# Larger DMA packets for the FFN weights in a fused attention and FFN kernel, with a new order of TensorE's work

## The chip, the cores and the metric

The kernel runs on one core of one Trainium2 chip. A core has five engines that run side by side and wait for each other through semaphores: TensorE (PE in the profile; its weight loads are listed as PEld) multiplies matrices, VectorE (DVE) and ScalarE (ACT) work element by element, GpSimd (POOL) does the same more slowly and also issues DMAs, and SyncE (SP) here issues DMAs only. Sixteen DMA engines move data between the chip's main memory and the on-chip memories. The metric is the device time of one execution in microseconds (us).

## What is computed

The reference, cut to what matters. Batch is 8, with 12 heads, 448 rows and 64 columns a head; d_model is 768 and d_ff 2048. The inputs are float32, and the kernel multiplies in bf16.

```python
def _attn_ref(q, k, v, w_pre, w_post):
    scale = 1.0 / np.sqrt(q.shape[-1])
    scores = scale * np.matmul(q, k.transpose(0, 1, 3, 2))
    scores = np.einsum('bhij,hg->bgij', scores, w_pre)
    scores = scores - np.max(scores, axis=-1, keepdims=True)
    attn = np.exp(scores)
    attn = attn / (np.sum(attn, axis=-1, keepdims=True) + 1e-09)
    attn = np.einsum('bhij,hg->bgij', attn, w_post)
    return np.matmul(attn, v).astype(np.float32)

def _moe_ref(x, w_in, w_out):
    h = np.maximum(x @ w_in, 0.0)
    return (h * h @ w_out).astype(np.float32)
```

The attention's output, 3584 rows (8 x 448) of 768 columns, is the `x` of the FFN.

## The kernel before

**Stages.** For each batch b the kernel transposes q and k on TensorE (T), multiplies them to scores (QK), copies the scores to `stage` on ACT or DVE, and has SP move them by DMA into `dring` (L875, one DMA for a chunk of 10 rows), in which the heads of 10 rows lie on the partitions. A matmul with `wk1` then mixes the heads (pre, L898), ACT takes the exponentials and their row sums (L915), DVE the reciprocals (L929), GpSimd folds them into the second mixing matrix `wk2s` (L936), and a second matmul mixes the heads again (post, L968), evacuated into `a2t`. After that come the product with v (AV, L1027, evacuated into `xt`), the first FFN matmul with `w_in_sb` (F1, L1075), relu (L1103, L1104) and square (L1113), and the second FFN matmul with `w_out_sb` (F2, L1192, and L1141 for the last two tiles), evacuated into `osb` and written out from GpSimd's queue (L1224).

The first 22 chunks of batch 0 skip the move through `dring`: DVE writes q, scaled by the head-mixing weights (L758), into the memory of `w_out_sb` (chunks 0 to 15) and of `h2t` (the others), and "direct" matmuls (L780) give the mixed scores at once. So w_out can be loaded only when the direct matmuls of chunks 0 to 15 are done.

**Queues.** GpSimd issues all loads of q, k (L585), v (L597) and the two weights (L623), because they convert float32 to bf16 on the way, and the output. `emit_load_w` (L607 to L633) issues the weights: i = 0 is w_in, i = 1 is w_out, each in four quarters j, and each quarter has a semaphore `sem_w[i][j]`. A quarter of w_in is 512 of its 2048 columns, issued as two DMAs of 256 columns over all six blocks of 128 rows. A quarter of w_out is four of its 16 blocks of 128 rows, issued as three DMAs of 256 of its 768 columns. An issue covers 128 partitions, and each (partition, block) pair is one run of 256 elements: 512 bytes in bf16. The first quarter of w_in is issued ahead of the loads of v for batch 0 and of q and k for batch 1, the other three behind them, w_out later among the folds. The list `chain` fixes the order of q, k and the weights on the queue; w_out's issues also stand behind certain pre units in the planner's order (`pre_at`).

**The order.** A planner in the kernel (class `_Plan`) decides, when the program is built, which engine does a task and in which order. TensorE's work is cut into 948 units in ten streams: 0 is T, 1 QK, 2 pre, 3 post, 4 AV, 5 direct, 6 and 7 F1, 8 and 9 F2. The string `ORDER` (L27) names, digit by digit, the stream from which TensorE takes its next unit, and within a stream the order is fixed. A position in this text is an index into that string, from 0. Each engine works strictly in its own order: an instruction that waits holds up all behind it. Where the planner expects a gap for TensorE in the first 60 us it fills part of it with matmuls on constant data that nothing reads (L554, "warm-up"). The planner knows DMAs by a rough model: the tuple `dma=(kind, work, packet)` gives a DMA's length and the time of one packet, both in ns, from which it works out how loads and moves slow each other (`dma_next`). Costs of instructions on an engine are tuples such as `{POOL: (850.0, 0.0)}`. These numbers set no time on the chip; they decide the order on the engines other than TensorE, and which of ACT and DVE evacuates.

Of the kernel before, what the change touches and what calls it, by code (L numbers as in the profile page):

```python
# [13 lines left out]
POOL = "pool"  # L14
# [10 lines left out]
DMA_END = {"move": 2800.0, "load": 2300.0}  # L25
INF = float("inf")
ORDER = (  # L27
    "0001510011055555555555155555513151555535533555555555335553200535555531155112555300333223"
    "1001244311412167663762727233636223717211636733221117433244226362717137637166116712276267"
    "3227933390120913922008122833833423811004111412283382238321812363637117261617337222444263"  # L30
    "3627173611671270022811833382238633673127442163672616733422767160002071718131812281382239"
    "1191339222919133933392244224193161336237117002261633737226126710027362126733702208183118"
    "1318223913911391339222442283381318331822244442136116227117163336227337220062236373117633"
    "6202071722009131911391139222838331833182224442219133931913392224442238138313831181162226"
    "7020273736126736211673372200623633713722009119113911192228183138333822281813382244444422"
    "8363162200732731631617131736222676376373372020821381244128382200911911191339339223922291"
    "9338118111833382224444233622617117362261761173362273376211673372193392229983338322882224"
    "44383338222838633667366776444776787667676767676876776798989988999988"
)


# [275 lines left out]
def bass_talking_heads_attention__then__ffn_squared_relu_kernel(  # L317
# [11 lines left out]
    F, FF = moe_w_in.shape  # L329
# [4 lines left out]
    NCH = -(-S // CH)  # L334
# [14 lines left out]
    NFT = F // 128  # L349
# [11 lines left out]
    with ExitStack() as es:  # L361
        def sb(name, shape, dtype):
            return es.enter_context(nc.sbuf_tensor(name, list(shape), dtype))
# [9 lines left out]
        NWP = 4  # L373
# [4 lines left out]
        WC = 256  # L378
# [13 lines left out]
        w_in_sb = sb("w_in_sb", [128, NFT, FF], DT.bfloat16)  # L392
        w_out_sb = sb("w_out_sb", [128, NFFT, F], DT.bfloat16)
# [212 lines left out]

        def emit_load_w(i, deps, quarters=range(NWP)):  # L607
            for j in quarters:
                nx = 2 if i == 0 else 3
                ts = w_of[(i, j)] = []  # L610
                for x in range(nx):
                    def fn(eng, en, j=j, x=x):
                        if i == 0:
                            c0 = j * (FF // NWP) + x * WC
                            src = bass.AP(moe_w_in.tensor, c0,
                                          [[FF, 128], [128 * FF, NFT], [1, WC]])
                            dst = w_in_sb[:, :, c0:c0 + WC]
                        else:
                            nt = NFFT // NWP
                            src = bass.AP(moe_w_out.tensor, j * nt * 128 * F + x * WC,  # L620
                                          [[F, 128], [128 * F, nt], [1, WC]])
                            dst = w_out_sb[:, j * nt:(j + 1) * nt, x * WC:(x + 1) * WC]
                        eng.dma_start(dst, src).then_inc(sem_w[i][j].handle, 16)  # L623

                    t = plan.add(
                        "ldw%d_%d_%d" % (i, j, x), POOL, fn, deps,
                        {POOL: (850.0 if i == 0 else 800.0, 0.0)},
                        (-2e5 if i == 0 and j == 0 else WPRIO + i) + j * 0.1, sem_w[i][j], 16,
                        after=[chain["t"]] + ([] if i == 0 else [
                            pre_at(min(24 + 2 * (3 * j + x), NCH - 1))]),  # L630
                        dma=("load", 2600.0 - 800.0 * i, 60.0))
                    chain["t"] = t
                    ts.append(t)  # L633

# [25 lines left out]
        def pre_at(g):  # L660
            return pre_of[g - g % NCP + g % NCP // 2 * 2]
# [574 lines left out]
        for b in range(B):  # L1236
            if b != 1:
                emit_load_qk(b)
            if b == 0:
                emit_load_w(0, [], range(1))  # L1240
            emit_T(b)
            if b == 0:
                t_wsmall = plan.add("wsmall", SP, fn_wsmall, [t_init, T_of[(0, 0, 0)]], {SP: (2600.0, 9500.0)}, -1e6,
                                    sem_w0, 48)

                t_wk1 = add("wk1", DVE, fn_wk1, [t_wsmall, t_mask], {DVE: (300.0, 400.0)}, -450.0)

                t_wk2 = add("wk2", DVE, fn_wk2, [t_wsmall, t_mask2], {DVE: (300.0, 400.0)}, -450.0)
                emit_load_qk(1)
                emit_load_w(0, [], range(1, NWP))  # L1250
                for a in range(3):
                    for c in range(NE):
                        emit_direct(c, (a, 3 + a))
                for c in range(0, NE - 1, 2):
                    emit_post(c)
                for c in range(NE, ND):
                    for ps_ in ((0, 1, 2), (3, 4, 5)):
                        emit_direct(c, ps_)
                    if c % 2:
                        emit_post(c - 1)  # L1260
# [8 lines left out]
            if b == 0:  # L1269
                emit_load_w(1, [dir_done[c] for c in range(NDW)])  # L1270
                emit_load_v(b)
            else:
                emit_load_v(b)
# [110 lines left out]
```

## Time and profile before

| What | Value |
|---|---|
| Three runs, us | 532.49, 532.8, 534.94 |
| Median, us | 532.8 |
| The profiled execution, us | 533.16 |
| Its span, first to last instruction, us | 531.4 |
| Granted TensorE clock | 1.000 |
| Loads of w_in: issues, KB each, median us from issue to landing | 8, 384, 16.0 |
| Loads of w_out: issues, KB each, median us from issue to landing | 12, 256, 8.1 |
| First and last issue of w_in, us | 10.1, 27.2 |
| First and last issue of w_out, us | 40.8, 67.9 |
| First matmul that reads w_in, us | 56.6 |
| First F2 matmul that reads w_out, us | 96.7 |
| Software DMA queue (all that GpSimd issues): packets, MB | 42816, 33.04 |
| Hardware DMA queue (moves into dring, last outputs): packets, MB | 45000, 36.86 |

Times within an execution count from the start of its span. Sizes are of the data as it is written, so in bf16 for the loads. The share of the DMA engines can pass 1, as packets of two queues overlap on one engine. "Issue" as the cause of a wait means that the engine waited for nothing that the profile shows; for TensorE that is mostly its own instructions, which are fetched by DMA in blocks of 16 KB (81 packets of the instruction queue).

### The profile page before, as it was taken

To read this page: it belongs to the slowest core of one execution; us is meant where nothing else is said; L and a number is where in the kernel's file an instruction comes from. 1 tells how busy PE (TensorE), PEld (TensorE's weight loads), DVE (VectorE), ACT (ScalarE), POOL (GpSimd) and SP (SyncE) were. 2 spreads that over 40 slices of the span, in tenths; PEclk is the share of its full clock that TensorE was granted. 3 is DMA by queue.
4 is the path that set the end of the run, shared out by engine and by line. 5 is a ranking of instruction groups with operands and counts; after the bars stand their busy time and mean duration, and the time that the engine had idled before them with its cause. 6 is when DMAs were issued, how large, how long until landed. Compare 5 with 4: busy or idle time off the path is not lost.

```text
span 531.4 us, 24004 instructions
## 1 busy us (share of the span) xinstructions
PE 514.6 (97%) x10033; PEld 321.2 (60%) x10033; DVE 401.0 (75%) x986; ACT 425.4 (80%) x1216; POOL 208.9 (39%) x404
## 2 busy tenths in 40 slices
PE   8999997899999999999989999999999999999997
PEld 3454765566767565566545665557655565567964
DVE  7986887788878769986879778986688777946530
ACT  4779997889989888979989988987979888986311
POOL 9933455332741256323641456213721333132000
PEclk9999999999999999999999999999999999999999
DMA  8999999755995379846993579727982558441003
GB/s 117 179 223 163 190 189 191 152 110 124 169 188 110 87 163 171 158 91 145 163 190 80 139 145 177 170 48 154 178 153 68 144 145 140 106 98 49 3 18 103
DMA packets 88210, 71.63 MB, mean 135 GB/s; under 512 B 13368, under 2 KB 85608, under 8 KB 88104
## 3 DMA queue, kind: packets, MB, share of 16 engines
q0 software_dynamic: 42816, 33.04, 39.9%
q1 hardware_dynamic: 45000, 36.86, 29.0%
q8 instruction: 81, 1.33, 1.0%
q10 hardware_dynamic: 288, 0.20, 0.1%
q14 instruction: 25, 0.20, 0.1%
HBM read 45.70 MB, written 11.01 MB: 107 GB/s over the span
## 4 chain that ended last, share of the span: by engine, by line
PE 88%; ACT 6%; DVE 2%; issue 2%; POOL 1%; DMA 1%; POOLq 0%; ACTq 0%
PE ps L1192 26%; PE ps L1075 26%; PE ps L968 8%; PE ps L898 8%; PE ps L1027 7%; PE ps L829 6%; PE ps L780 4%; ACT pring L915 3%; PE ps L683 2%; PE ps L1141 2%; ACT stage L447 1%; DMA qraw<-in_q_dram 1%; ACT a2t L447 1%; POOL qraw L585 1%; DVE a2t L448 1%
## 5 line engine op out<-in xcount | busy, mean ns | idle before, releaser
L915 ACT ACTIVATE pring<-ps 128x448 bf16<-128x448 f32 x360 | 191.4, 556 | 15.1 <-PE ps L898 8.4
L1075 PE MATMUL ps<-xt,w_in_sb 64*128 64x448 bf16 (+2 forms) x2112 | 167.3, 299 | 3.0 <-issue 1.6
L936 POOL TENSOR_TENSOR wk2s<-wk2b,rinv 128x120 bf16<-128x120 bf16 (+1 forms) x179 | 71.6, 403 | 212.7 <-DVE rinv L929 212.1
L1192 PE MATMUL ps<-w_out_sb,h2t 64*128 64x384 bf16 x1664 | 151.3, 323 | 1.2 <-DVE h2t L1113 1.2
L448 DVE CAST a2t<-ps 128x480 bf16<-128x480 f32 (+1 forms) x197 | 120.5, 639 | 21.4 <-PE ps L968 20.6
L1075 PEld LDWEIGHTS ps<-xt,w_in_sb 64*128 64x128 bf16 x2112 | 94.8, 94 | 53.1 <-issue 5.7
L448 DVE CAST stage<-ps 128x448 bf16<-128x448 f32 (+1 forms) x177 | 106.6, 618 | 16.7 <-PE ps L829 14.7
L447 ACT ACTIVATE stage<-ps 128x448 bf16<-128x448 f32 (+1 forms) x183 | 95.5, 554 | 18.7 <-PE ps L829 17.7
L1192 PEld LDWEIGHTS ps<-w_out_sb,h2t 64*128 64x128 bf16 x1664 | 77.3, 94 | 51.2 <-issue 1.5
L447 ACT ACTIVATE a2t<-ps 128x480 bf16<-128x480 f32 (+1 forms) x171 | 91.5, 577 | 18.6 <-PE ps L968 18.2
L915 ACT ACTIVATION_READ_ACCUMULATOR pring<-ps 128x1 f32 x360 | 79.5, 221 | 0.0
L1224 POOL DMA_DIRECT2D out_dram<-osb x52 | 33.6, 652 | 95.4 <-ACT pring L915 47.1
L968 PEld LDWEIGHTS ps<-wk2s,pring 60*128 60x128 bf16 x2880 | 55.7, 93 | 23.4 <-issue 4.5
L968 PE MATMUL ps<-wk2s,pring 60*128 60x60 bf16 x2880 | 62.1, 187 | 1.8 <-issue 0.8
L1104 DVE TENSOR_SCALAR h1t<-ps 128x448 bf16<-128x448 f32 (+2 forms) x95 | 45.7, 491 | 17.6 <-PE ps L1075 16.8
L929 DVE RECIPROCAL rinv<-rowsum 128x2 f32<-128x2 f32 (+1 forms) x184 | 29.0, 158 | 33.8 <-ACT pring L915 33.4
L829 PE MATMUL ps<-qkt 64*128 64x448 bf16 (+1 forms) x360 | 51.4, 354 | 3.0 <-issue 2.3
L898 PE MATMUL ps<-dring,wk 64*64 64x448 bf16 (+1 forms) x676 | 53.2, 363 | 0.7 <-DVE a2t L448 0.2
L1113 DVE TENSOR_TENSOR h2t<-h1t 128x448 bf16<-128x448 bf16 (+2 forms) x176 | 51.7, 330 | 2.3 <-ACT h1t L1103 2.0
L1103 ACT ACTIVATE h1t<-ps 128x448 bf16<-128x448 f32 (+2 forms) x81 | 36.4, 451 | 19.5 <-PE ps L1075 17.4
L1027 PE MATMUL ps<-a2t,vraw 128*64 128x220 bf16 (+1 forms) x768 | 41.1, 260 | 0.0
L1027 PEld LDWEIGHTS ps<-a2t,vraw 128*64 128x64 bf16 x768 | 35.8, 109 | 5.8 <-ACT osb L447 2.1
(50 smaller groups left out, 366.7 us busy)
## 6 DMA issues: line engine op xcount, KB each, us to landing
dring<-stage SPq DMA_DIRECT2D x309, 105.0 KB
out_dram<-osb POOLq DMA_DIRECT2D x52, 192.0 KB, 4.0
qraw<-in_q_dram POOLq DMA_DIRECT2D x48, 112.0 KB, 5.2
kraw<-in_k_dram POOLq DMA_DIRECT2D x48, 112.0 KB, 5.7
w_in_sb<-in_moe_w_in_dram POOLq DMA_DIRECT2D x8, 384.0 KB, 16.0
vraw<-in_v_dram POOLq DMA_DIRECT2D x24, 128.0 KB
w_out_sb<-in_moe_w_out_dram POOLq DMA_DIRECT2D x12, 256.0 KB, 8.1
vraw<-in_v_dram POOLq DMA_DIRECT2D x24, 96.0 KB
```

What stands on the lines that cost most here:

```text
L447: return eng.activation(o, i_, AF.Copy)
L448: return eng.tensor_copy(o, i_)
L829: r_ = eng.matmul(ps[y * w:(y + 1) * w, g.banks[x], 0:S], qkt[r0:r0 + 64, pb, p + y, 0, i0:i0 + w], qkt[r0:r0 + 64, pb, p + y, 1, :], star ...
L898: r_ = eng.matmul(ps[64 * y:64 * y + 64, gr.banks[x], 0:S], wk1[64 * x:64 * x + 64 - R0 * x, :], dring[64 * x:64 * x + 64 - R0 * x, (g0 + ...
L915: return eng.activation(pring[:, pr, 0:S], ps[:, gr.banks[x], 0:S], AF.Exp, accum_out=rowsum[:, pr, :])
L936: return eng.tensor_tensor(wk2s[:, p0:p0 + n, :], i0.to_broadcast([128, n, PR]), rinv[:, p0:p0 + n, :].to_broadcast([128, n, PR]), ALU.mult)
L968: r_ = eng.matmul(ps[:, gr.banks[x], o0:o0 + PR], pring[64 * x:64 * x + PR, pr + y, j0:j0 + 2 * PJ], wk2s[64 * x:64 * x + PR, pr + y, :], ...
L1027: r_ = eng.matmul(ps[kk * 64:kk * 64 + 64, g.banks[0], x * n:(x + 1) * n], vraw[:, h, s, :], a2t[half][:, s, h, a0:a0 + n], start=(s == 0) ...
L1075: r_ = eng.matmul(ps[:, g.banks[x], 0:n], w_in_sb[64 * y:64 * y + 64, ft, t * 128:(t + 1) * 128], xt[64 * y:64 * y + 64, ft, c0:c1], start ...
L1104: return eng.tensor_scalar(h1t[:, s, 0:n], ps[:, g.banks[x], 0:n], 0.0, None, op0=ALU.max)
L1113: return eng.tensor_tensor(h2t[:, t16, o0:o0 + n], h1t[:, s, 0:n], h1t[:, s, 0:n], ALU.mult)
L1192: r_ = eng.matmul(ps[:, g.banks[hh], 0:FH], h2t[64 * y:64 * y + 64, t16, col:col + 128], w_out_sb[64 * y:64 * y + 64, t16, hh * FH:(hh + 1 ...
```

## The change

`emit_load_w` cuts the weights another way. A quarter of w_in is still two DMAs, but each takes three of the six blocks of 128 rows with all 512 columns of the quarter: runs of 1024 bytes, 384 in an issue instead of 768. A quarter of w_out is two DMAs of 384 columns instead of three of 256: runs of 768 bytes, 512 in an issue as before, eight issues instead of twelve. The planner's numbers for these DMAs change with it, and so does the spacing of the pre units behind which w_out's issues stand. `ORDER` is replaced by another string, found by a search for these loads; it has the same number of units of each stream. Its first two and its last lines are shown, and of the eight lines between them nearly all differ in some places.

```diff
 ORDER = (
-    "0001510011055555555555155555513151555535533555555555335553200535555531155112555300333223"
-    "1001244311412167663762727233636223717211636733221117433244226362717137637166116712276267"
...
-    "44383338222838633667366776444776787667676767676876776798989988999988"
+    "0005500551505155555555555511155153355331151555555531315555002555355555533155520530233321"
+    "1002441334123616217637262327373117376162216613732142274433326267176136731771611622762267"
...
+    "44383338222863336673676767764446777677686787676767767689989999888989"
 )
...
             for j in quarters:
-                nx = 2 if i == 0 else 3
+                nx = 2
+                wc = WC if i == 0 else 384
                 ts = w_of[(i, j)] = []
                 for x in range(nx):
-                    def fn(eng, en, j=j, x=x):
+                    def fn(eng, en, j=j, x=x, wc=wc):
                         if i == 0:
-                            c0 = j * (FF // NWP) + x * WC
-                            src = bass.AP(moe_w_in.tensor, c0,
-                                          [[FF, 128], [128 * FF, NFT], [1, WC]])
-                            dst = w_in_sb[:, :, c0:c0 + WC]
+                            c0, nr = j * (FF // NWP), NFT // 2
+                            src = bass.AP(moe_w_in.tensor, x * nr * 128 * FF + c0,
+                                          [[FF, 128], [128 * FF, nr], [1, FF // NWP]])
+                            dst = w_in_sb[:, x * nr:(x + 1) * nr, c0:c0 + FF // NWP]
                         else:
                             nt = NFFT // NWP
-                            src = bass.AP(moe_w_out.tensor, j * nt * 128 * F + x * WC,
-                                          [[F, 128], [128 * F, nt], [1, WC]])
-                            dst = w_out_sb[:, j * nt:(j + 1) * nt, x * WC:(x + 1) * WC]
+                            src = bass.AP(moe_w_out.tensor, j * nt * 128 * F + x * wc,
+                                          [[F, 128], [128 * F, nt], [1, wc]])
+                            dst = w_out_sb[:, j * nt:(j + 1) * nt, x * wc:(x + 1) * wc]
                         eng.dma_start(dst, src).then_inc(sem_w[i][j].handle, 16)
 
                     t = plan.add(
                         "ldw%d_%d_%d" % (i, j, x), POOL, fn, deps,
-                        {POOL: (850.0 if i == 0 else 800.0, 0.0)},
+                        {POOL: (700.0, 0.0)},
...
                         after=[chain["t"]] + ([] if i == 0 else [
-                            pre_at(min(24 + 2 * (3 * j + x), NCH - 1))]),
-                        dma=("load", 2600.0 - 800.0 * i, 60.0))
+                            pre_at(min(24 + 3 * (2 * j + x), NCH - 1))]),
+                        dma=("load", 2250.0, 99.0 - 23.0 * i))
```

More of the change, by code (lines that the diff above doesn't have):

```diff
@@ L27 @@
 ORDER = (
-    "0001510011055555555555155555513151555535533555555555335553200535555531155112555300333223"
-    "1001244311412167663762727233636223717211636733221117433244226362717137637166116712276267"
[L30 to L37, printed above, removed]
-    "44383338222838633667366776444776787667676767676876776798989988999988"
+    "0005500551505155555555555511155153355331151555555531315555002555355555533155520530233321"
+    "1002441334123616217637262327373117376162216613732142274433326267176136731771611622762267"
+    "3722923932193001920038122833822381143004111142383238322831833616171172261763373242244223"
+    "6613717163167172020822183382238363736372124442363671167672276160000271718111833382228939"
+    "1139111932391229333922442243931631161002711733622267337621167020276321673372002833811183"
+    "1382229391139133922244422381118313831382224442336136227137161116223737202062236373117633"
+    "6220071720209111911391339222838331833822244422191119133933392224442218118133813833271622"
+    "6736202063711276216733372620206117333702209119139113922283811383118222831833382244444422"
+    "8363316200273611732671371631662226733773370202444211838122831820029191119133932293392229"
+    "1191383813183138222444223611671317162226731763336722276116733721933922293938338222838224"
+    "44383382228863336673367676776444677677686787676767767689989999888989"
 )
```

## The prediction

> **What bounds the kernel now.** First the page's busy times and its chain that ended last:
>
> ```profile
> PE 514.6 (97%) x10033; PEld 321.2 (60%) x10033; DVE 401.0 (75%) x986; ACT 425.4 (80%) x1216; POOL 208.9 (39%) x404
> ...
> PE 88%; ACT 6%; DVE 2%; issue 2%; POOL 1%; DMA 1%; POOLq 0%; ACTq 0%
> ```
>
> TensorE works 97% of the span, and 88% of the chain is its own work; DMA holds 1%. Any saving must therefore come out of the 16.7 us (531.4 - 514.6) in which TensorE stands, or out of its warm-up matmuls. Then the busy time by stage, to see where those 16.7 us lie (columns: window, length, busy us and instructions of PE, PEld, DVE, ACT, POOL, granted clock, DMA share, GB/s):
>
> ```profile
> 0.00:57.00 57.00, 53.69 (x859) 27.01 (x861) 48.00 (x114) 42.89 (x113) 36.91 (x63) 1.00 1.14 172
> 57.00:110.00 53.00, 46.70 (x1048) 33.39 (x1044) 40.87 (x120) 44.05 (x134) 25.47 (x48) 1.00 0.96 176
> ...
> 110.00:520.00 410.00, 406.44 (x8097) 256.29 (x8092) 312.14 (x754) 336.47 (x966) 146.53 (x293) 1.00 0.62 125
> 520.00:532.00 12.00, 7.82 (x49) 4.50 (x46) 0.00 (x0) 1.96 (x4) 0.00 (x0) 0.99 0.34 89
> ```
>
> Idle: 3.3 us before 57 us, 6.3 us from 57 to 110, only 3.6 us in the 410 us after that, and the tail. The weights are loaded between 10 and 80 us, and there the DMA engines are full (share about 1). So I looked at what TensorE waits for between 44 and 100 us:
>
> ```profile
> PE ps L829 <- issue: 2.3, 1, 2.3
> ...
> PE ps L1192 <- DVE h2t L1113: 1.2, 1, 1.2
> PE ps L1075 <- ACT pring L915: 1.1, 1, 1.1
> ...
> PE ps L968 <- POOL wk2s L936: 0.7, 2, 0.5
> ```
>
> No line names a weight load or a move into dring: data from DMA is in time. The waits are for TensorE's own instruction supply (issue), exponentials, evacuations. Last, TensorE's timeline at the one place where it fills a gap with warm-ups (L554):
>
> ```profile
> 46.60 0.55 PE L554 MATMUL ps<-warm 128*128 128x448 bf16 x2
> 47.42 0.84 PE L968 MATMUL ps<-wk2s,pring 60*128 60x60 bf16 x48 [0.26 <-POOL wk2s L936]
> 48.19 0.84 PE L898 MATMUL ps<-dring,wk 64*64 64x448 bf16 x8
> 49.03 1.31 PE L554 MATMUL ps<-warm 128*128 128x448 bf16 x6
> 50.80 0.40 PE L968 MATMUL ps<-wk2s,pring 60*128 60x60 bf16 x16 [0.47 <-POOL wk2s L936]
> ```
>
> **The change part by part.** The sum is made against the profiled execution, 533.16 us (span 531.4 and 1.8 around it), 0.36 above the median of 532.8.
>
> *Packets.* In the trace's packet records a 512-byte packet of the software queue takes 60 ns, one of 896 bytes 88, one of 384 bytes 51: about 23 ns plus 0.072 ns a byte, so I estimate 97 ns for 1024 bytes and 78 for 768. w_in: 6144 packets x 60 = 369 us of packet time become 3072 x 97 = 298; w_out: 369 become 4096 x 78 = 319. Saved: 121 us, over 16 engines 7.5 us of a full DMA system. On the end: 0. What hides it: w_in's last issue is at 27.2 us and its landings take 7.3 to 22.1 us, while the first matmul that reads it (L1075) is at 56.6; w_out's last issue is at 67.9, its landings take at most 13.6, and its first reader (L1192) is at 96.7. The margins are 7 and 15 us; were they gone, the DMA saving would count at most those 7.5 us.
>
> *Issues on GpSimd.* w_in's issues (768 descriptors each) take a median of 1.04 us, w_out's (512) 0.78, those of q (128) 0.63. Between the last two a 384-descriptor issue costs about 0.72: 8 x 0.32 = 2.5 us less, and four w_out issues fewer, 4 x 0.78 = 3.1 us less. Behind them on this queue stand v, q and k of batch 1, then the folds (L936), which wait 212 us in all for the reciprocals and not for the queue. Counted at 0; without that cover 5.6 us.
>
> *Order, start.* Before, two QK units stand ahead of T1k and one direct unit; now four direct units (positions 3, 4, 7, 8) come early and most QK units of batch 0's first tile go back, its last from position 29 to 31. The loads still release the transposes (the waits at 10.5 and 12.3 us). The direct units fill part of a warm-up (0.36) and of a 0.2 us wait: bounds 0 and -0.6, I take **-0.4**, as nearly all of that stretch waits for DMA anyhow.
>
> *Order, 46 to 51 us.* The post unit that waits at 50.80 (the 14th, at position 87) moves to 95, behind two AV units; a pre unit is pulled ahead. Gap and warm-ups are 0.55 + 0.26 + 1.31 + 0.47 = 2.6 us. Bounds 0 and -2.6; I take half, **-1.3**, since ACT is busy 33.3 of the 35 us from 45 to 80 and cannot deliver much sooner. For the same reason part is given back where TensorE next waits for ACT (0.8 us at 72 to 73, 1.05 at 81): bounds 0 and +1.7, I take **+0.9**.
>
> *Order, batch 1's moves.* The last QK unit of batch 1's first tile goes from position 101 to 105, behind two more F1 units and a pre unit: 2 x 0.67 + 0.3 = 1.6 us later, and SP's moves (L875) of that tile wait for its evacuation. By the semaphore events the moves land 1.1 us apart beside the weight loads. Pre units need pairs of them; before, they came 5.0, 3.5, 5.2, 5.0, 3.0 and 2.8 us after their data. Their positions shift by +2, +4, -3, +1, +2, +17, at some 0.5 us each. If the spacing stays 1.1, none is caught; if it grows with the packet (78/60, 1.44), the fifth pair's slack is 3.0 - 1.6 + 1.0 - 10 x 0.34 = -1.0. Faster moves would gain nothing, as none is waited for. Bounds 0 and +2 (the third pair caught as well); I take **+0.7**.
>
> *Instruction supply.* Waits named issue (2.3 at 86.7 us, 1.6 at 272 us, 0.8, 0.6) fall where many short instructions meet busy DMA; a new order throws them anew. Bounds -4 and +4, taken as 0.
>
> *The rest of the order.* From position 180 on each unit stands within a few places of where it was (up to position 250 the counts by stream differ by one at most); with 3.6 us idle there, 0 is taken.
>
> Sum: -0.4 - 1.3 + 0.9 + 0.7 = -0.1, so 533.1 us; against the median 532.7. I forecast **533.0 us**, no change: within 0.5% (2.7 us, about what a measurement of this kernel can tell from no change). Its own range is 530.3 to 535.7.
>
> **The rivals.**
> *Slower by the moves (chance 0.22).* Between 27 and 36 us both queues run at once (columns: packets, MB, share of 16 engines):
>
> ```profile
> q0 software_dynamic: 2318, 1.29, 101.3%
> q1 hardware_dynamic: 823, 0.69, 30.0%
> ```
>
> The two streams share the engines, and a move's packet that comes behind a longer load packet may wait longer for its turn. If the spacing follows the 1024-byte packet (97/60, 1.78 us), the fifth pair is 3.0 - 1.6 + 1.0 - 10 x 0.68 = 4.4 us late; TensorE takes its work in order, so the F1 and post units behind wait too, and ACT, with 1.7 us free from 45 to 80, can't make it up. Instead of +0.7 stands +4.4: 536.8. It decides once the spacing passes about 1.35 us. For it: the slack of 3 us and the later start of the moves. Against: before, no move is waited for, and the loads are over sooner. [...]
>
> *Slower by the later order (0.16).* 110 to 520 us has 3.6 us idle in 410, so a new order can hardly gain there and can lose: two more waits for instructions of 2 us (the mean of the 2.3 and 1.6 seen) make 537.0. Against: the order is nearly the old one.
>
> *Faster (0.18).* The 2.6 us at 46 to 51 go whole, nothing is given back, and the 2.3 us at 86.7 vanish because the loads that keep DMA busy then end some us earlier: 533.16 - 0.4 - 2.6 - 2.3 = 527.9. Half of the last two gives 530.3, the edge of the forecast. Against: ACT's 95%.
>
> *The packets don't change*, if runs are split anyway: 60 ns and 512 bytes stay; the time is that of the forecast, whose chance of 0.44 includes it.
>
> **How the numbers follow.** Faster 0.18; same 0.44; slower 0.22 + 0.16 = 0.38. The range leaves out about half of the faster case and a quarter of the two slower ones: 529.0 to 538.0.
>
> **What would show it.** Packet records of 1024 and 768 bytes at 97 and 78 ns; w_in issues near 0.72 us, eight of w_out; w_in and w_out landed as far ahead of L1075 and L1192 as before; fewer L554 matmuls between 46 and 51 us; no wait of L898 for dring. A wait of L898 behind DMA, or landings more than 1.35 us apart, means the first rival; more than 6 us idle between 110 and 520 us the second; no wait at L829 near 87 us and the first F1 matmul before 55 us the third. A TensorE total idle that falls or grows by over 3 us would make the forecast wrong.

## The result, and the profile after

| | Before | After |
|---|---|---|
| Median of 22 runs each, us | 532.44 | 535.94 |
| Range of those runs, us | 528.56 to 534.94 | 532.27 to 541.54 |
| The profiled execution, us | 533.16 | 537.38 |
| Its span, us | 531.4 | 535.6 |

The changed kernel is slower by 0.62%: the ratio of after to before is 1.0062, with a 95% interval of 1.0039 to 1.0085. Slow executions (three of the 22 after) are left out of all ratios, and the profiles of two trials that fell on slow executions (the new order with the old packets, and w_out earlier) are left out wherever profiles are counted by order.

The page after, busy times, DMA queues and the chain:

```profile
PE 516.5 (96%) x10031; PEld 322.0 (60%) x10031; DVE 400.2 (75%) x979; ACT 428.8 (80%) x1223; POOL 204.0 (38%) x400
...
q0 software_dynamic: 37632, 33.04, 38.4%
...
PE 81%; DVE 7%; DMA 5%; ACT 3%; issue 2%; POOL 1%; SPq 0%; ACTq 0%; DVEq 0%
```

The packets did change: 5184 fewer for the same megabytes (of them 3072 fewer for w_in and 2048 fewer for w_out), and 39.9% of the engines' time became 38.4%. The packet records show 98 ns at the median for 1024 bytes and 79 for 768, where I had estimated 97 and 78. But the span grew by 4.2 us and DMA stands on the chain with 5% instead of 1%. By stage (columns as before):

```profile
0.00:57.00 57.00, 52.53 (x831) 25.97 (x833) 44.71 (x108) 41.50 (x110) 33.64 (x62) 1.00 1.04 171
57.00:110.00 53.00, 46.08 (x1030) 32.41 (x1026) 41.67 (x120) 44.87 (x134) 22.75 (x45) 1.00 0.89 170
110.00:520.00 410.00, 405.81 (x8099) 256.71 (x8096) 313.32 (x753) 340.11 (x975) 145.18 (x291) 1.00 0.62 125
```

The 410 us from 110 on are nearly as they were (4.2 us idle, 3.6 before). Nearly everything is lost ahead of them: by 110 us TensorE has run 46 matmuls fewer (1861 against 1907), and the first F1 matmul starts at 60.4 us instead of 56.6. From the fifth F2 unit on, F2's matmuls start 2.4 to 5.2 us later than their counterparts, apart from a few that the order displaces, and the last ones 4.3 us later; nothing is made up. TensorE's waits up to 115 us, after:

```profile
PE ps L969 <- issue: 2.9, 2, 2.0
PE ps L899 <- DMA dring<-stage: 1.7, 3, 0.8
PE ps L1076 <- issue: 1.6, 1, 1.6
...
PE ps L684 <- issue: 1.2, 1, 1.2
```

Lines have moved by one: L969 is the post matmul, L899 pre, L1076 F1, L684 T. Waits for TensorE's own instructions make 5.7 us here, against 2.9 before (the 2.3 at 86.7 us and 0.6), and waits for the moves into dring, of which there were none, make 1.7. The timeline in front of F1:

```profile
53.54 0.19 PE L684 MATMUL ps<-ident,qraw 64*64 64x64 bf16 x1 [1.24 <-issue]
53.54 0.41 PE L684 MATMUL ps<-ident,kraw 64*64 64x64 bf16 x28
53.88 0.38 PE L899 MATMUL ps<-dring,wk 64*64 64x448 bf16 x4
54.19 1.70 PE L1028 MATMUL ps<-a2t,vraw 128*64 128x220 bf16 x32
55.82 0.36 PE L830 MATMUL ps<-qkt 64*128 64x448 bf16 x2
56.02 0.61 PE L969 MATMUL ps<-wk2s,pring 60*128 60x60 bf16 x32
56.56 0.94 PE L1028 MATMUL ps<-a2t,vraw 128*64 128x220 bf16 x16
57.43 0.36 PE L830 MATMUL ps<-qkt 64*128 64x448 bf16 x2
57.73 0.38 PE L899 MATMUL ps<-dring,wk 64*64 64x448 bf16 x4
58.04 0.23 PE L969 MATMUL ps<-wk2s,pring 60*128 60x60 bf16 x3
60.26 0.36 PE L969 MATMUL ps<-wk2s,pring 60*128 60x60 bf16 x13 [1.99 <-issue]
```

Both waits break a unit in the middle (27 of 28 transposes, 35 of 48 post matmuls), where no operand can be missing: what is missing are instructions. Between them lie 124 matmuls in 4.7 us. The whole execution has 10031 matmuls and 81 blocks, 124 a block, so with their weight loads they are about one block of instructions. The packet records of the instruction queue fit: a block's packet starts at 51.22, 57.91 and 69.93 us, each ends 1.1 to 1.4 us before TensorE goes on (at 53.54, 60.26 and 72.56). The same holds for every longer wait named issue: the fourteen profiles of this case have 61 of more than 0.5 us, and in each of them a block's packet had ended 0.9 to 1.7 us before TensorE went on.

Two theories were to be told apart. **Packets**: longer load packets hold up the moves into dring, and what waits for these is late. **Order**: the new sequence of TensorE's units loses by itself, through instruction waits and new gaps. All ratios below are to the kernel before, run on the same chip, with 95% intervals. The trials were run on three chips, so compare them by their ratios and not by their times.

### The profile page after: what moved, and what is told of

It reads as the page before. It is cut to its first block, busy times and chain, and to the rows that moved or that the text cites. A ratio compares the mean times of both kernels' runs of the same rounds, so it can differ in the third digit from the quotient of the medians.

```text
span 535.6 us, 23972 instructions
## 1 busy us (share of the span) xinstructions
PE 516.5 (96%) x10031; PEld 322.0 (60%) x10031; DVE 400.2 (75%) x979; ACT 428.8 (80%) x1223; POOL 204.0 (38%) x400
## 3 DMA queue, kind: packets, MB, share of 16 engines
q0 software_dynamic: 37632, 33.04, 38.4%
## 4 chain that ended last, share of the span: by engine, by line
PE 81%; DVE 7%; DMA 5%; ACT 3%; issue 2%; POOL 1%; SPq 0%; ACTq 0%; DVEq 0%
PE ps L1193 25%; PE ps L1076 23%; PE ps L969 7%; PE ps L899 7%; PE ps L1028 6%; DMA dring<-stage 5%; PE ps L830 5%; DVE w_out_sb L759 3%; PE ps L1142 2%; PE ps L684 2%; PE ps L781 2%; DVE stage L448 1%; ACT pring L916 1%; PE ps L554 1%; ACT stage L447 1%
## 5 line engine op out<-in xcount | busy, mean ns | idle before, releaser
L1076 PE MATMUL ps<-xt,w_in_sb 64*128 64x448 bf16 (+2 forms) x2112 | 165.9, 299 | 1.9 <-issue 1.6
L448 DVE CAST a2t<-ps 128x480 bf16<-128x480 f32 (+1 forms) x209 | 127.3, 639 | 23.2 <-PE ps L969 22.1
L1076 PEld LDWEIGHTS ps<-xt,w_in_sb 64*128 64x128 bf16 x2112 | 94.9, 94 | 50.0 <-issue 4.1
L447 ACT ACTIVATE stage<-ps 128x448 bf16<-128x448 f32 (+1 forms) x194 | 100.8, 554 | 22.2 <-PE ps L830 19.9
L448 DVE CAST stage<-ps 128x448 bf16<-128x448 f32 (+1 forms) x166 | 100.3, 618 | 17.0 <-PE ps L830 14.8
L447 ACT ACTIVATE a2t<-ps 128x480 bf16<-128x480 f32 (+1 forms) x159 | 84.9, 572 | 13.4 <-PE ps L969 12.9
L916 ACT ACTIVATION_READ_ACCUMULATOR pring<-ps 128x1 f32 x360 | 78.4, 218 | 0.0
L969 PEld LDWEIGHTS ps<-wk2s,pring 60*128 60x128 bf16 x2880 | 56.8, 93 | 27.3 <-issue 5.9
L969 PE MATMUL ps<-wk2s,pring 60*128 60x60 bf16 x2880 | 63.6, 187 | 4.9 <-issue 3.1
L899 PE MATMUL ps<-dring,wk 64*64 64x448 bf16 (+1 forms) x676 | 53.9, 363 | 3.2 <-DMA dring<-stage 2.7
L1104 ACT ACTIVATE h1t<-ps 128x448 bf16<-128x448 f32 (+2 forms) x91 | 39.1, 441 | 17.2 <-PE ps L1076 14.1
L830 PE MATMUL ps<-qkt 64*128 64x448 bf16 (+1 forms) x360 | 50.0, 353 | 0.6 <-ACT a2t L447 0.2
L1105 DVE TENSOR_SCALAR h1t<-ps 128x448 bf16<-128x448 f32 (+2 forms) x85 | 41.8, 500 | 11.2 <-PE ps L1076 10.0
```

Source lines behind the costliest of these rows:

```text
L447: return eng.activation(o, i_, AF.Copy)
L448: return eng.tensor_copy(o, i_)
L830: r_ = eng.matmul(ps[y * w:(y + 1) * w, g.banks[x], 0:S], qkt[r0:r0 + 64, pb, p + y, 0, i0:i0 + w], qkt[r0:r0 + 64, pb, p + y, 1, :], star ...
L899: r_ = eng.matmul(ps[64 * y:64 * y + 64, gr.banks[x], 0:S], wk1[64 * x:64 * x + 64 - R0 * x, :], dring[64 * x:64 * x + 64 - R0 * x, (g0 + ...
L916: return eng.activation(pring[:, pr, 0:S], ps[:, gr.banks[x], 0:S], AF.Exp, accum_out=rowsum[:, pr, :])
L969: r_ = eng.matmul(ps[:, gr.banks[x], o0:o0 + PR], pring[64 * x:64 * x + PR, pr + y, j0:j0 + 2 * PJ], wk2s[64 * x:64 * x + PR, pr + y, :], ...
```

## The experiments

**One: the change taken apart.** Four kernels. The first is the kernel before with w_in alone in the new packets:

```diff
-                            c0 = j * (FF // NWP) + x * WC
-                            src = bass.AP(moe_w_in.tensor, c0,
-                                          [[FF, 128], [128 * FF, NFT], [1, WC]])
-                            dst = w_in_sb[:, :, c0:c0 + WC]
+                            c0, nr = j * (FF // NWP), NFT // 2
+                            src = bass.AP(moe_w_in.tensor, x * nr * 128 * FF + c0,
+                                          [[FF, 128], [128 * FF, nr], [1, FF // NWP]])
+                            dst = w_in_sb[:, x * nr:(x + 1) * nr, c0:c0 + FF // NWP]
```

> The kernel before with w_in alone in 1024-byte packets; every engine keeps its old sequence of instructions. If longer packets alone cost the 3.5 us, by moves into dring that land 1.5 us apart instead of 1.1, part of the loss shows here: slower by 1 us or more, 533.5 us and up. If the order costs them, the slack of 3 to 5 us ahead of each pre unit covers the later moves and the time stays within 0.8 us of 532.4. Both: moves beside w_in land 1.4 to 1.6 us apart, w_in's issues near 0.75 us.

Measured: 528.91 us, ratio 0.9961 (0.9933 to 0.9989). Not slower but a little faster. w_in's issues took 0.94 us at the median (1.04 before). The moves beside w_in did slow down: in the run of moves from the fifth to the tenth, one landed every 1.59 us, where before it was 1.12. TensorE waited for dring not once.

The second is the changed kernel with the old order:

```diff
 ORDER = (
-    "0005500551505155555555555511155153355331151555555531315555002555355555533155520530233321"
+    "0001510011055555555555155555513151555535533555555555335553200535555531155112555300333223"
...
 )
```

> The changed kernel with the old ORDER: both packets, the new numbers of the planner. Packets at fault: 535 us or more, with TensorE waiting for dring at L899. Order at fault: within 1 us of 532.4, no wait of L899 for dring over 0.3 us.

Measured: 529.79 us, ratio 0.9978 (0.9952 to 1.0003). TensorE's waits up to 115 us:

```profile
PE ps L554 <- DVE warm L539: 1.5, 1, 1.5
PE ps L684 <- DMA qraw<-in_q_dram: 0.8, 2, 0.4
PE ps L684 <- DMA kraw<-in_k_dram: 0.8, 2, 0.6
PE ps L969 <- POOL wk2s L937: 0.7, 2, 0.5
PE ps L899 <- issue: 0.7, 1, 0.7
```

No line names dring, although the moves land 1.58 us apart beside w_in here (the fifth to the tenth again): in this kernel the old order has slack for it. Instruction waits add up to 0.9 us.

The third is the kernel before with the new order, its packets and planner numbers left as they were:

```diff
 ORDER = (
-    "0001510011055555555555155555513151555535533555555555335553200535555531155112555300333223"
+    "0005500551505155555555555511155153355331151555555531315555002555355555533155520530233321"
...
 )
```

> The kernel before with the new ORDER, its packets of 512 bytes and its old planner numbers. Packets at fault: within 1 us of 532.4. Order at fault: 535 to 537 us, with the first F1 matmul (L1075) near 60 us as in the changed kernel. Both together at fault (the order leans on the moves, the packets delay them): between, 533.5 to 535.

Measured: 536.04 us, ratio 1.0082 (1.0049 to 1.0115). The order alone costs what the whole change costs, or slightly more; 0.9978 x 1.0082 is 1.0060, close to the measured 1.0062.

The fourth was meant to be the changed kernel with both weights in 512-byte packets. w_in got its old access patterns back, w_out this:

```diff
-                            src = bass.AP(moe_w_out.tensor, j * nt * 128 * F + x * wc,
-                                          [[F, 128], [128 * F, nt], [1, wc]])
-                            dst = w_out_sb[:, j * nt:(j + 1) * nt, x * wc:(x + 1) * wc]
+                            src = bass.AP(moe_w_out.tensor, (j * nt + 2 * x) * 128 * F,
+                                          [[F, 128], [128 * F, 2], [WC, 3], [1, WC]])
+                            dst = w_out_sb[:, j * nt + 2 * x:j * nt + 2 * x + 2, :].rearrange(
+                                "p a (b c) -> p a b c", c=WC)
```

> The changed kernel with both weights in 512-byte packets, in as many issues as the change has; every other instruction stands where it stood. Packets at fault: back near 532.4, moves 1.1 us apart, no wait of L899 for dring. Order at fault: 535 to 536.5, as the changed kernel. A share of each: the waits of L899 for dring (2.7 us in the changed kernel) go and the waits for instructions (5.7 us up to 110 us) stay, 534 us.

Measured: 538.02 us, ratio 1.0132 (1.0082 to 1.0182). The edit did not do what its label says: the three runs of 256 columns touch, they were merged, and the packet records show w_out in 2048 packets of 1536 bytes, 135 ns each. So it is the opposite trial for w_out, its packets doubled against the change. Moves of batch 1's first tile land 1.9 us apart beside them (from the 26th to the 30th move), and then TensorE waits (L900 is the pre matmul in this kernel):

```profile
PE ps L900 <- DMA dring<-stage: 3.4, 1, 3.4
```

What the first rival reckoned with can happen, then: at 1536 bytes in the new order the moves land 1.9 us apart and TensorE waits 3.4 us for one.

**Two: where in the order.** At position 99 both orders have taken the same number of units of each stream, so they can be joined there. Both kernels keep the changed packets and planner numbers. `old` and `new` stand for the two strings.

```diff
-ORDER = new
+ORDER = old[:99] + new[99:]
```

> The changed kernel (its packets, its planner numbers) with the first 99 positions of the old ORDER and the new one from there; at 99 both have taken the same units of each stream. Theory 'start': the new order loses before the first F1, where short units run TensorE out of instructions, and the later waits for dring follow from that lateness; then 529 to 531 us, as with the whole old order. Rival 'rest': the later positions wait for dring and for instructions by themselves; then 533 to 536 us.

```diff
-ORDER = new
+ORDER = new[:99] + old[99:]
```

> The mirror: the first 99 positions of the new ORDER, then the old one. Theory 'start': 532.5 us or more, the first F1 matmul near 60 us with instruction waits of 3 us before it. Rival 'rest': within 1 us of the 529.8 of the whole old order.

Measured: old start 532.61 us, ratio 1.0035 (1.0010 to 1.0060); new start 534.81 us, ratio 1.0077 (1.0045 to 1.0110). Against 0.9978 with the old order throughout, the new start costs 1.0% and the new rest 0.6%. Neither theory of the expectation holds alone. The two add up to more than the 0.84% between the whole new order and the whole old one with these packets (1.0062 and 0.9978). That would fit if a delay in the start hid part of what the rest would wait for, but no run shows it. The profile of old start and new rest has one long wait for instructions:

```profile
70.87 0.50 PE L1077 MATMUL ps<-xt,w_in_sb 64*128 64x220 bf16 x4 [2.53 <-issue]
```

The kernel with the new start shows what became of the gap between 46 and 51 us (its lines stand one further down than in the changed kernel):

```profile
33.76 0.40 PE L970 MATMUL ps<-wk2s,pring 60*128 60x60 bf16 x16 [0.56 <-POOL wk2s L938]
34.08 0.36 PE L555 MATMUL ps<-warm 128*128 128x448 bf16 x1
...
37.62 0.74 PE L555 MATMUL ps<-warm 128*128 128x448 bf16 x3
...
48.88 0.55 PE L555 MATMUL ps<-warm 128*128 128x448 bf16 x2
49.75 0.84 PE L970 MATMUL ps<-wk2s,pring 60*128 60x60 bf16 x48 [0.32 <-POOL wk2s L938]
...
51.21 0.36 PE L831 MATMUL ps<-qkt 64*128 64x448 bf16 x2 [0.26 <-ACT a2t L448]
51.56 0.36 PE L555 MATMUL ps<-warm 128*128 128x448 bf16 x1
52.08 0.36 PE L831 MATMUL ps<-qkt 64*128 64x448 bf16 x2 [0.16 <-ACT pring L917]
...
53.48 0.19 PE L685 MATMUL ps<-ident,qraw 64*64 64x64 bf16 x1 [0.69 <-issue]
```

The whole old order with the same packets has the three warm-ups at 37 us too, and those at 49 us and the wait for a fold behind them have their like there at 47.72 and 48.53; it does not have the gap at 33 us:

```profile
36.84 0.74 PE L554 MATMUL ps<-warm 128*128 128x448 bf16 x3
```

So the six warm-ups (1.31 us) and the wait of 0.47 us of the old order are gone, and what stands in their place is a wait for a fold (0.56) with a warm-up at 33 us, two waits for ACT (0.26 and 0.16) with a warm-up between them, and two waits for instructions (0.69, and 0.67 at 59.3). In the profiles, TensorE stands 5.5 to 7.5 us ahead of the first F1 matmul with the new start (six kernels) and 3.3 to 5.0 with the old one (the kernel before and five others); F1 begins at 58.4 to 60.6 us and at 56.2 to 58.4. The profiled execution of the new start took 532.65 us, 2.2 less than the median, so it shows only part of what the median pays; the last section has more of it.

**Three: the queue in front of the instruction blocks.** The changed kernel with w_out's issues moved back, so that none is queued when the first block comes late:

```diff
-                            pre_at(min(24 + 3 * (2 * j + x), NCH - 1))]),
+                            pre_at(30 + 2 * (2 * j + x))]),
```

> The changed kernel with w_out's eight issues moved behind later pre units (30, 32, ... 44 instead of 24, 27, ... 44), so that no weight load is queued from about 45 to 55 us; TensorE's order is the same. If TensorE's instruction blocks come late because they queue behind these loads, the two waits at 53.5 and 60.3 us (3.2 us) fall below 1 us and the time to 533 to 534. If the new order simply uses instructions up faster than they can come, both waits stay and the time is 535 to 537.

Measured: 541.48 us, ratio 1.0173 (1.0117 to 1.0229), the slowest of all. The first w_out issue came at 50.9 us instead of 45.4. The wait at 53.5 us was gone, and F1 began 1.4 us sooner (59.0); the second wait stayed (1.75 us at 58.8). Then eight loads lay in 19 us, and 3.9 us were lost at 86 us in a wait for a fold:

```profile
86.16 0.40 PE L969 MATMUL ps<-wk2s,pring 60*128 60x60 bf16 x16 [3.94 <-POOL wk2s L937]
```

That one of the two waits went would fit load in front of an instruction block delaying it, but the time did not fall. The mirror, with w_out earlier:

```diff
-                            pre_at(min(24 + 3 * (2 * j + x), NCH - 1))]),
+                            pre_at(22 + 3 * (2 * j + x))]),
```

> The changed kernel with w_out's issues behind pre units 22, 25, ... 43 instead of 24, 27, ... 44: the mirror of h3_wout_later (541.5), which pressed the eight loads into less time. If what costs is the crowd of loads between 64 and 80 us, beside the moves that the pre units need, spreading them gains: 533 to 535. If the two instruction waits at 53.5 and 60.3 us come from loads that are queued in front of the instruction blocks, more load there makes them worse: 536 to 538.

Measured: 536.46 us, ratio 1.0107 (1.0070 to 1.0144), against the changed kernel's 1.0062 (1.0039 to 1.0085): no gain, and too near to tell a loss. In its profile the wait at 53 us is down to 0.16 us, though w_out's loads start 5.8 us earlier (at 39.6 us), and the one at 60 us is 2.24. The first wait shrank both ways, then, so that load in the queue delays the blocks is not shown.

**Four: each weight's packets by itself, in both orders.** The kernel before with w_out alone in the new packets, then with both (the first diff of this section added):

```diff
-                nx = 2 if i == 0 else 3
+                nx = 2
...
-                            src = bass.AP(moe_w_out.tensor, j * nt * 128 * F + x * WC,
-                                          [[F, 128], [128 * F, nt], [1, WC]])
-                            dst = w_out_sb[:, j * nt:(j + 1) * nt, x * WC:(x + 1) * WC]
+                            src = bass.AP(moe_w_out.tensor, j * nt * 128 * F + x * FH,
+                                          [[F, 128], [128 * F, nt], [1, FH]])
+                            dst = w_out_sb[:, j * nt:(j + 1) * nt, x * FH:(x + 1) * FH]
...
-                            pre_at(min(24 + 2 * (3 * j + x), NCH - 1))]),
+                            pre_at(min(24 + 3 * (2 * j + x), NCH - 1))]),
```

> The kernel before with w_out alone in 768-byte packets, eight issues; all engines but GpSimd keep their old sequence. w_in's packets alone gave 0.9961. If what helps is that the loads of weights, v, q and k are through earlier when TensorE fetches instructions near 87 us, w_out's packets, which stand nearer to that place, help as well: 528.5 to 530.5 us. If w_in's gain has another cause, 531 to 532.5.

> The kernel before with both weights in the new packets, old ORDER and old planner numbers, all engines but GpSimd with their old sequence: the change without its order. If the packets' effects add (0.9961 and 1.0001), 0.996 of the kernel before, near 529; if w_out's longer packets take back what w_in's give, 0.999 to 1.003.

Measured: w_out alone 531.58 us, ratio 1.0001 (0.9972 to 1.0030); both 531.28 us, ratio 1.0009 (0.9979 to 1.0039). With 0.9961 for w_in alone and 0.9978 for both with the new planner numbers, the packets under the old order are worth somewhere between nothing and 0.4%. w_in's gain did not show again with both, but those two intervals overlap (0.9933 to 0.9989, 0.9979 to 1.0039) and the runs were on different chips, so that something takes it back is not shown either. The profile with both has a wait that the other kernels of the old order do not have, and 2.1 us of waits for instructions:

```profile
PE ps L898 <- DMA dring<-stage: 1.1, 1, 1.1
```

So the old order's slack for the moves can run out too.

In the new order, the changed kernel with w_out back in 512-byte packets (two DMAs where x is 0, and the semaphore's increment set for both), and the changed kernel with w_in back in 512-byte packets (its old access patterns):

```diff
-                            src = bass.AP(moe_w_out.tensor, j * nt * 128 * F + x * wc,
-                                          [[F, 128], [128 * F, nt], [1, wc]])
-                            dst = w_out_sb[:, j * nt:(j + 1) * nt, x * wc:(x + 1) * wc]
+                            for y in range(2 * x, 2 + x):
+                                src = bass.AP(moe_w_out.tensor, j * nt * 128 * F + y * WC,
+                                              [[F, 128], [128 * F, nt], [1, WC]])
+                                dst = w_out_sb[:, j * nt:(j + 1) * nt, y * WC:(y + 1) * WC]
+                                eng.dma_start(dst, src).then_inc(sem_w[i][j].handle, 16)
+                            return
```

> The changed kernel with w_out in 512-byte packets again (two issues where it has one, one where it has one, so twelve); every other instruction stands as in the changed kernel. If w_out's longer packets hold up the moves of batch 1's first tile (1.4 us apart; 2.0 beside the 1536-byte packets of e5_after_512, which was 538.0), moves come 1.1 us apart here, the waits of L899 for dring (2.7 us) go and the time is 533 to 535. If the order alone costs the time, 535 to 537.

> The changed kernel with w_in in 512-byte packets again, in as many issues; all else as changed. If w_in's longer packets gain in the new order as they did in the old one (0.9961), this is slower than the changed kernel, 537 to 539. If they hurt there through the moves of batch 0's tile, 533.5 to 535. If they don't matter, 535 to 537.

Measured: w_out back 536.42 us, ratio 1.0098 (1.0064 to 1.0132); w_in back 537.60 us, ratio 1.0134 (1.0081 to 1.0187). Neither brings the time back. Up to 115 us the waits of pre for dring were zero in both, and the instruction waits 5.0 and 4.1 us. The moves' delay is therefore not the main cost in the changed kernel; the order is, with any packets that were tried. Over the profiles, instruction waits up to 115 us are 4.0 to 5.7 us with the whole new order (five kernels) and 0.9 to 2.9 with the whole old one (five).

The lowest ratio of these has the kernel before with w_in alone in 1024-byte packets, 0.9961, 0.39% under the kernel before; the interval of the one with both packets and the new planner numbers (0.9978) overlaps with it.

## Why the prediction was right or wrong

The forecast of no change did not hold: 535.94 us lies inside the wide range, but 0.2 us above the forecast's own, and the change cost 0.62% where at most 0.5% was forecast. The case that came about is "slower". That the wide range holds the time owes more to its width than to the sum, whose terms for the order came out differently one by one:

- *Packets, issues on GpSimd: 0.* Right. The packet times came within 1 ns, w_in's and w_out's last landings stayed ahead of their first readers (48.8 against 60.4 us, 84.1 against 97.9), and the whole packet change under the old order measured 0.9978 to 1.0009. w_in's issues were mis-sized: they took 0.93 us at the median, not 0.72. The descriptors alone do not set the time: both before and after, the first two issues were shorter (0.84 and 0.76 us) than the six that follow each other closely (1.04 and 0.94). Nothing on TensorE's path was seen to wait for it.
- *Start, -0.4, and 46 to 51 us, -1.3.* Wrong, and the main failure. "I take half" looked at the one gap that the old order has and not at those that the new order opens: by F1 the new start is 1.7 us behind the old one with the same packets (59.4 against 57.7), where -1.7 in all had been counted. About half of that is lost by the two warm-ups at 48 us (48.88 against 47.72, of which some 0.3 is the pre unit that moved ahead of them) and the rest behind them.
- *Given back at ACT, +0.9.* Did not come: TensorE's waits for ACT from 55 to 115 us were 1.7 us before and are 0.4 after. TensorE got there later, and waited for instructions instead.
- *Instruction supply, 0.* Mis-sized: 5.7 us in place of 2.9 up to 115 us. The range of -4 to +4 held it; the value did not. All five profiles of the new order show more of it than any of the old one, so it is no chance draw, as I treated it, but belongs to that order.
- *Batch 1's moves, +0.7.* 1.7 us of waits at L899 up to 115 us and 1.1 after. The spacing moved nearly as priced: 1.35 us beside w_out (1.44 assumed) and 1.57 beside w_in (1.78 was named). The delay of the moves was mis-sized: the first move of batch 1 is issued at 64.0 us instead of 57.9, 6.1 us later where 1.6 were counted, since the start was late as well. But where those waits were taken away up to 115 us, the time did not fall, so they seem to cover other lateness.
- *The rest of the order, 0.* Wrong: +0.6% by itself, with the old start. Its profile shows the wait for instructions of 2.5 us at 68 to 71 us, and right behind it F1's matmuls take longer (twelve of them 1.31 us at 71.54, 0.73 at 75.97); the granted clock is 0.97 over 57 to 110 us (an estimate: 0.03 x 53, 1.6 us more). That this is what the median pays is not shown.
- *Rivals.* "Slower by the moves": part of its spacing came, its price did not, except with packets of 1536 bytes. The spacing beside w_in, on which it reckoned, never met batch 1's moves: w_in's last load had landed at 48.8 us, and the first of these moves lands at 67. Why moves land further apart beside longer load packets no run shows, only that they do (in the old order 1.59 us beside w_in's 1024 bytes, 1.12 beside its 512). "Slower by the later order" had the right cause, more waits for instructions, at the wrong place: they lie before 115 us, and from 110 to 520 us idle time is 4.2 us, not over 6. Of "Faster" only the wait at 87 us came, which is gone.

What stays open: how much of the instruction waits is the pace of short units and how much the loads in the queue (both trials that moved w_out's loads shortened the first wait and kept the second), how the new order's loss divides between instruction waits, new gaps and the lower granted clock, and whether w_in's packets alone gain more than both.

## What to carry to other kernels

A new order of a full engine is a change of its own: run it with the old data movement, and the movement with the old order, before the two are judged together. Saved DMA time was worth little here, where TensorE hardly waited for DMA: between nothing and 0.4% under the old order. An order found on a model can trade one visible gap for several small ones that the model doesn't hold, such as the supply of instructions (here 5.7 us of waits in place of 2.9 up to 115 us), so count the matmuls between such waits (here 124 in 4.7 us).

## What the runs showed of the hardware

In several profiles a wait of 1.75 us or more was followed by a stretch of lower granted clock. The trial with w_out later, in windows around its instruction wait at 58.8 us (the clock stands third from the end):

```profile
55.00:59.00 4.00, 2.25 (x70) 1.52 (x63) 2.82 (x5) 3.11 (x9) 0.90 (x2) 1.00 1.00 189
59.00:63.00 4.00, 4.00 (x57) 2.65 (x50) 2.83 (x8) 2.68 (x8) 1.13 (x2) 0.57 0.81 134
63.00:67.00 4.00, 4.00 (x96) 2.96 (x94) 2.94 (x10) 3.32 (x11) 3.00 (x5) 1.00 1.02 148
```

At a mean clock of 0.57, 57 matmuls run in 4 us where 96 run in the next 4, and twelve of F1's take 1.35 us (at 59.88) where they take 0.73 at 63.87. So behind the wait of 1.75 us up to 1.7 us more were lost (an estimate: 0.43 x 4.00). With w_out in packets of 1536 bytes the wait of 3.43 us up to 83.22 was followed by 0.79 from 85 to 90 us, after 0.86 from 80 to 85 (an estimate: 0.14 x 5 + 0.21 x 5, 1.75 us). It is not certain: the 2.0 us in the changed kernel and the 2.3 us in the kernel before were not followed by one (1.00 from 57 to 110 us in both). What lowers the clock no run shows.

The unprofiled executions have their mean granted clock on record too. One such stretch, 1.7 us by the estimate, is 0.32% of 532 us. The profile of old start and new rest, with 0.97 from 57 to 110 us and 1.00 before that and from 110 to 500, has a clock of 0.997. With the new start, a clock of 0.997 or less stands beside 53 of 81 executions, with the old start (the kernel before included) beside 35 of 140. For new start and old rest this goes with the time: the four executions at 1.0 have a median of 532.1 us, the other eight of 535.9. For the changed kernel it hardly does (535.3 us at 0.999 or more, 536.1 at 0.997 or less), so the lower clock can be only a part of what the new order costs.
